# One pool of SBUF slots for the pieces of two weight matrices, with new orders for all engines

## The chip, the cores and the metric

The kernel runs on one core of one Trainium2 chip. A core has engines that each work through their own list of instructions in order: the tensor engine (PE), the vector engine (DVE), the scalar engine (ACT), GpSimd (POOL) and SyncE (SP), which in this kernel issues every DMA. The metric is the device time of the program in microseconds (us), lower is better. The kernel before took 477.4 us in the median of 6 runs, 476.62 to 478.06.

## The reference

Two layers with the same weights. A layer is attention over a sliding window, then an MLP that mixes along the sequence. All arrays are bf16; the sequence has 2048 rows, the model width is 512.

```python
def _A_ref(x, wqkv, wo):                       # D 512, 32 heads of 16, window 256
    qkv = (x @ wqkv).reshape(B, S, 3, H, Dh) ...
    scores = einsum("bhqd,bhkd->bhqk", q, k) * Dh ** -0.5
    mask = (idx[:, None] - idx[None, :] >= 0) & (idx[:, None] - idx[None, :] < W)
    p = softmax(where(mask, scores, -1e9))
    return einsum("bhqk,bhkd->bhqd", p, v) ... @ wo

def _B_ref(x, w1, b1, w2, b2):                 # w1 2048 x 1792, w2 1792 x 2048
    u = gelu(einsum("bsd,sf->bdf", layernorm(x), w1) + b1)
    y = einsum("bdf,fs->bds", u, w2) + b2
    return y.transpose(0, 2, 1)

x = A_x
x = x + _A_ref(layernorm(x), A_wqkv, A_wo)
x = x + _B_ref(layernorm(x), B_w1, B_b1, B_w2, B_b2)
...                                            # and both lines once more
```

## The kernel before

**Stages.** The sequence is cut in four chunks of 512 rows. `STEPS` (L258) lists the stages of each layer: `p` prepares a chunk (layer norm, in layer 1 also the last MLP's output rows it starts from, then q, k and v), `a` is its attention, `w` the output projection `wo`, `u` a part of the MLP's first product, `U` that product's last part with the gelu, and the `y` blocks are the second product (in layer 0 they are taken in by the next layer's `p`, in layer 1 they end the program, each followed by the DMA of its rows to the output).

**Attention** (`attention`, L903). PE makes scores in PSUM (L925); ACT takes their exponential into one of eight buffers `pt` (L937); DVE multiplies a mask in (L950, L953); PE multiplies with v (L971). DVE copies the product and the sums of a group of heads to a buffer `cs` (L1015). SP then brings the sums together (`rr`, L1017), moves half the product to the lower partitions (`cs`, L1021), and after DVE's reciprocal (L1024) writes it to DRAM (`rscr`, L1026) and reads it back spread over partitions (`md`, L1029). POOL multiplies both into `oT` (L1033), which `wo_block` (L1039) takes. The last group of each layer goes another way, with ACT (L998, L1000) and DVE (L1002). POOL also prepares k for the scores (`kbd`, L857).

**Layer norm** (`ln_block`, L753). DVE takes statistics (L757, L759), POOL the reciprocal deviation (L762, L764), DVE normalises to `xh_sb` (L768). PE transposes are read out by L803.

**The MLP.** `u_part` (L1075) multiplies pieces of w1 with `xh_sb` (L1089). A piece of w1 is 512 rows by 256 columns, 256 KB, loaded by `load_w1` (L1056, the DMA is L1058) to one of the four buffers of `w1b`. Its sum goes from PSUM to `ub` by a copy (L1098) for the first part of the sequence, by an addition (L1101) for later ones; gelu is L1104. `y_block` (L1109) multiplies pieces of w2 with the result (L1112); L1117 adds bias and residual. A piece of w2 is 256 rows by 256 columns, 128 KB, loaded by `load_w2` (L1064, the DMA is L1069) to one of the fourteen buffers of `w2b`, with at most 3 (layer 0) or 7 (layer 1) such loads under way.

**What sets the order.** Every step of this is recorded as an operation by `op` of the class `Graph` (L289), with what it reads and writes. `ORDER` (L21) holds one list of operation numbers for each engine, written out by hand or by a search. `follow` (L423) walks the five lists and gives each tile a slot of its pool, the moment an operation needs one; `reorder` (L493) then applies the small shifts of `MOVES` (L166), and `emit` (L502) writes each engine's instructions in that order with the semaphore waits that data and slots need. A list is strictly in order: an instruction that waits holds up all behind it on its engine, and a DMA that waits for a buffer holds up all later DMAs, since SP has a single list.

The two weight buffers take 8 KB and 14 KB of each partition:

```python
        w1b = sb("w1b", [P, NW1, 4, 256])                  # NW1 is 4
        w2b = sb("w2b", [P, 2 * NFT // W2F, W2F, 256])     # 14 buffers
...
        p_w1, p_w2, p_rscr = Pool("w1", NW1), Pool("w2", 2 * NFT // W2F), Pool("rscr", 3)
```

Of the kernel before, what the change touches and what calls it, by code (L numbers as in the profile page):

```python
# [11 lines left out]
P = 128  # L12
# [4 lines left out]
W2F, W2OUT = 2, (3, 7)  # L17
# [5 lines left out]
        11, 6, 13, 9, 14, 17, 10, 5, 16, 15, 8, 7, 69, 12, 71, 84, 85, 75, 73, 87, 77, 78, 81, 82, 93, 88, 185, 94,  # L23
        103, 104, 110, 96, 97, 111, 90, 91, 190, 100, 33, 107, 101, 108, 137, 195, 133, 114, 115, 135, 149, 200,
        139, 150, 217, 158, 152, 153, 222, 159, 205, 141, 227, 142, 155, 156, 232, 161, 162, 249, 254, 237, 166,
        146, 167, 147, 259, 169, 170, 174, 264, 175, 182, 183, 281, 177, 178, 329, 286, 331, 559, 333, 335, 561,
        291, 578, 269, 579, 296, 342, 343, 413, 337, 338, 366, 417, 367, 374, 375, 421, 425, 301, 563, 557, 356,
        429, 357, 351, 352, 445, 361, 362, 382, 449, 573, 574, 383, 453, 457, 433, 461, 570, 369, 370, 571, 477,
        481, 388, 389, 385, 465, 485, 386, 394, 489, 395, 391, 392, 493, 609, 610, 509, 606, 607, 513, 517, 497,
        653, 646, 654, 647, 521, 656, 657, 663, 525, 664, 593, 594, 743, 614, 615, 747, 529, 751, 588, 589, 755,  # L30
        345, 346, 348, 759, 349, 583, 584, 775, 565, 566, 779, 763, 783, 670, 671, 787, 598, 599, 649, 791, 650,
        677, 678, 807, 623, 624, 795, 811, 377, 378, 617, 667, 815, 618, 668, 819, 681, 682, 620, 823, 621, 601,
        602, 839, 626, 627, 843, 827, 847, 674, 675, 688, 851, 689, 684, 685, 855, 691, 692, 660, 948, 661, 702,
        703, 952, 705, 706, 859, 956, 712, 719, 720, 713, 960, 716, 717, 698, 964, 699, 726, 980, 727, 709, 968,
        984, 710, 730, 733, 734, 988, 731, 723, 992, 724, 880, 881, 996, 737, 738, 874, 1012, 875, 1016, 1000, 1020,
        740, 741, 695, 1024, 696, 871, 872, 1028, 877, 878, 1044, 1048, 1032, 1052, 1056, 900, 901, 917, 918, 1060,
        907, 908, 910, 911, 914, 924, 925, 903, 904, 915, 1064, 1065, 921, 922, 931, 928, 929, 1069, 1070, 932, 938,
        939, 1072, 1073, 935, 936, 1075, 1076, 1078, 945, 1079, 942, 1122, 946, 943, 1116, 1103, 1109, 1117, 1104,
        1129, 1123, 1110, 1135, 1124, 1130, 1131, 1105, 1106, 1111, 1118, 1112, 1136, 1137, 1119, 1125, 1148, 1138,
        1142, 1132, 1149, 1143, 1150, 1144, 1145, 1151, 1273, 1268, 1255, 1181, 1161, 1155, 1162, 1163, 1182, 1156,  # L40
        1183, 1164, 1168, 1157, 1169, 1170, 1158, 1187, 1184, 1171, 1174, 1175, 1269, 1176, 1177, 1274, 1188, 1189,
        1190, 1256, 1270, 1275, 1276, 1271, 1250, 1257, 1258, 1251, 1252, 1253, 1292, 1326, 1327, 1308, 1309, 1290,
        1288, 1328, 1286, 1302, 1303, 1294, 1314, 1321, 1297, 1316, 1406, 1299, 1305, 1300, 1306, 1319, 1311, 1411,
        1324, 1329, 1344, 1416, 1345, 1346, 1421, 1331, 1438, 1347, 1332, 1443, 1333, 1334, 1426, 1448, 1349, 1350,
        1453, 1351, 1470, 1352, 1362, 1475, 1376, 1458, 1377, 1480, 1364, 1485, 1379, 1380, 1366, 1534, 1502, 1368,
        1535, 1392, 1507, 1370, 1490, 1374, 1512, 1536, 1394, 1537, 1517, 1385, 1386, 1382, 1642, 1383, 1398, 1646,
        1400, 1522, 1650, 1404, 1388, 1654, 1539, 1540, 1658, 1541, 1542, 1674, 1552, 1662, 1678, 1553, 1554, 1572,
        1682, 1555, 1557, 1686, 1570, 1558, 1690, 1559, 1560, 1706, 1584, 1585, 1587, 1710, 1588, 1694, 1714, 1576,
        1574, 1620, 1718, 1612, 1606, 1722, 1610, 1604, 1738, 1600, 1582, 1742, 1746, 1726, 1622, 1578, 1750, 1590,
        1591, 1595, 1596, 1754, 1618, 1624, 1938, 1775, 1776, 1942, 1777, 1778, 1946, 1770, 1758, 1950, 1771, 1772,  # L50
# [4 lines left out]
        2169, 1900, 1904, 2173, 1901, 2189, 1911, 2177, 2193, 1912, 2066, 2197, 2070, 1916, 2201, 1917, 1919, 1920,  # L55
        2205, 2068, 2072, 2221, 1908, 1909, 2225, 2229, 2209, 1927, 1928, 2233, 1924, 1925, 2237, 1932, 1933, 1935,
        1936, 2241, 2242, 2091, 2093, 2103, 2101, 2096, 2250, 2246, 2252, 2113, 2111, 2108, 2248, 2106, 2098, 2118,
        2116, 2123, 2121, 2276, 2282, 2277, 2283, 2278, 2279, 2284, 2285, 2289, 2295, 2290, 2291, 2292, 2296, 2297,
        2298, 2315, 2316, 2321, 2322, 2317, 2318, 2323, 2308, 2309, 2302, 2303, 2310, 2304, 2311, 2324, 2334, 2305,
        2328, 2329, 2330, 2335, 2336, 2347, 2337, 2422, 2348, 2440, 2331, 2341, 2428, 2349, 2342, 2434, 2360, 2423,  # L60
        2343, 2354, 2361, 2355, 2350, 2356, 2429, 2344, 2441, 2362, 2363, 2435, 2452, 2424, 2357, 2436, 2446, 2430,
        2453, 2431, 2447, 2442, 2425, 2458, 2464, 2443, 2459, 2465, 2437, 2454, 2448, 2470, 2466, 2460, 2476, 2455,
        2477, 2471, 2461, 2449, 2467, 2478, 2472, 2479, 2488, 2473, 2482, 2483, 2489, 2490, 2484, 2500, 2501, 2494,
        2502, 2491, 2506, 2495, 2503, 2496, 2485, 2507, 2508, 2497, 2509, 2512, 2513, 2514, 2515,
    ),
    (
# [542 lines left out]
def bass_interleave_layers__sliding_block__mixer_token_mlp__prompt_kernel(  # L609
# [16 lines left out]
    NFT = F // P  # L626
# [4 lines left out]
    with es:  # L631
        sb = lambda name, shape, d=dt.bfloat16: es.enter_context(nc.sbuf_tensor(name, shape, d))
# [18 lines left out]
        w1b = sb("w1b", [P, NW1, 4, 256])  # L651
# [535 lines left out]
```

## Time and profile before

| what | us |
|---|---|
| median of 6 runs | 477.4 |
| the profiled execution | 477.06 |
| its span, first to last instruction | 475.3 |
| PE busy | 427.2 |
| DVE busy | 369.4 |
| ACT busy | 326.1 |
| POOL busy | 127.8 |
| share of 16 DMA engines that SP's queue used | 36.1% |

The mean granted clock of the tensor engine was 0.999. Busy time by stretch of the span:

| us of the span | length | PE | DVE | ACT | POOL | DMA share |
|---|---|---|---|---|---|---|
| 20 to 160 | 140 | 118.54 | 126.51 | 129.94 | 52.37 | 0.30 |
| 160 to 213 | 53 | 49.29 | 41.25 | 22.95 | 10.28 | 0.39 |
| 213 to 300 | 87 | 82.48 | 68.97 | 77.29 | 20.05 | 0.30 |
| 300 to 350 | 50 | 43.48 | 46.44 | 42.00 | 23.65 | 0.28 |
| 350 to 396 | 46 | 41.06 | 34.44 | 34.88 | 11.52 | 0.43 |
| 396 to 475 | 79 | 75.17 | 35.59 | 9.49 | 4.36 | 0.49 |

How to read it: an engine that is busy for nearly the whole of a stretch bounds it. In a group of the profile the name before the arrow is the output, the name behind it the input, L is the line of the kernel, and the idle time before an instruction is put down to what released it. A wait of an engine that is not on the chain costs nothing by itself.

### The profile page before, as it was taken

What the parts mean: (1) busy time and instruction counts of PE and PEld (TensorE: products, weight loads), DVE (VectorE), ACT (ScalarE), POOL (GpSimd) and SP (SyncE); (2) the same over time, 40 slices, a digit from 0 to 9 for tenths busy, and PEclk for the clock granted to TensorE, in tenths of its full rate; (3) what the DMA queues carried; (4) which work ended last, traced back from release to release, by engine and by line L of the source; (5) the groups of instructions that cost most, each with busy time, mean ns of one, the idle gap of its engine ahead of it and who ended that gap; (6) DMA issues with size and microseconds to landing.
All of it is one profiled execution on the core that took longest, in us unless ns stands there. A gap on an engine that the chain in (4) does not pass through costs nothing.

```text
span 475.3 us, 15635 instructions
## 1 busy us (share of the span) xinstructions
PE 427.2 (90%) x6764; PEld 206.6 (43%) x6830; DVE 369.4 (78%) x747; ACT 326.1 (69%) x371; POOL 127.8 (27%) x189
## 2 busy tenths in 40 slices
PE   7989877789887799999989998989978979999996
PEld 4454433354343344445454454445434434444442
DVE  7999979889988989574789888989985986941332
ACT  1999999799988951528998898888778862033000
POOL 3151454325612222010002714530591031200000
PEclk9999999999999999999999999999999999999999
DMA  8311431132443434331133513512316335533563
GB/s 243 91 51 48 110 118 50 49 92 64 127 122 108 138 115 121 102 101 34 36 99 77 139 41 106 147 51 51 83 51 178 98 109 171 146 98 113 165 192 130
DMA packets 83993, 49.47 MB, mean 104 GB/s; under 512 B 14676, under 2 KB 78164, under 8 KB 83924
## 3 DMA queue, kind: packets, MB, share of 16 engines
q1 hardware_dynamic: 83924, 48.46, 36.1%
q8 instruction: 54, 0.88, 0.8%
q14 instruction: 15, 0.12, 0.1%
HBM read 41.43 MB, written 2.59 MB: 93 GB/s over the span
## 4 chain that ended last, share of the span: by engine, by line
PE 61%; ACT 19%; DVE 13%; issue 2%; DMA 2%; POOL 1%; SPq 0%; POOLq 0%
PE PS L1112 18%; ACT pt L937 18%; PE PS L1089 16%; PE PS L836 5%; PE PS L925 5%; PE PS L971 5%; PE PS L1043 5%; PE PS L871 4%; DVE xh_sb L768 2%; DVE pt L950 2%; DVE cs L1015 2%; DVE pt L953 2%; PE PS L686 1%; DMA w1b<-in_B_w_dram 1%; DVE x_sb L1117 1%
## 5 line engine op out<-in xcount | busy, mean ns | idle before, releaser
L937 ACT ACTIVATE pt<-PS 128x1024 bf16<-128x1024 f32 (+1 forms) x304 | 283.4, 1038 | 30.8 <-PE PS L925 28.3
L1089 PE MATMUL PS<-xh_sb,w1b 128*128 128x512 bf16 x424 | 103.3, 380 | 9.8 <-ACT pt L937 2.5
L1112 PE MATMUL PS<-ub,w2b 128*128 128x512 bf16 x431 | 100.9, 379 | 1.8 <-issue 1.1
L925 PE MATMUL PS<-qT,kbd 32*128 32x64 bf16 (+4 forms) x1632 | 60.8, 243 | 19.1 <-ACT pt L937 8.1
L1089 PEld LDWEIGHTS PS<-xh_sb,w1b 128*128 128x128 bf16 x448 | 39.9, 98 | 58.8 <-issue 6.9
L1112 PEld LDWEIGHTS PS<-ub,w2b 128*128 128x128 bf16 x448 | 41.6, 98 | 51.3 <-issue 3.9
L1101 DVE TENSOR_TENSOR ub<-PS,ub 128x512 f32<-128x512 f32 x70 | 45.6, 683 | 22.9 <-PE PS L1089 22.8
L836 PE MATMUL PS<-xhT,wqkv 128*128 128x512 bf16 x238 | 59.5, 380 | 2.9 <-issue 2.2
L857 POOL TENSOR_SCALAR kbd<-stg,par 128x512 bf16<-128x512 bf16 x48 | 41.2, 869 | 69.8 <-DVE stg L803 69.6
L1033 POOL TENSOR_TENSOR oT<-cs,md 128x512 bf16<-128x512 f32 x30 | 40.3, 1346 | 69.1 <-DMA cs<-cs 49.2
L953 DVE TENSOR_TENSOR pt<-pt,ldm 128x1024 bf16<-128x1024 bf16 (+1 forms) x80 | 56.4, 714 | 2.6 <-ACT pt L937 2.6
L925 PEld LDWEIGHTS PS<-qT,kbd 32*128 32x128 bf16 x1632 | 23.3, 92 | 75.0 <-ACT pt L937 42.5
L1104 ACT ACTIVATE ub<-ub,bcol 128x512 bf16<-128x512 f32 x28 | 18.5, 712 | 46.7 <-DVE ub L1101 46.6
L1015 DVE COPY cs<-PS 128x512 f32<-128x512 f32 x60 | 38.8, 682 | 12.2 <-PE PS L971 11.9
L1117 DVE SCALAR_TENSOR_TENSOR x_sb<-PS,bcol,x_sb 128x512 bf16<-128x512 f32 x32 | 23.2, 745 | 31.2 <-PE PS L1112 31.1
L950 DVE TENSOR_TENSOR pt<-pt,ldm 128x512 bf16<-128x512 bf16 (+1 forms) x104 | 40.8, 413 | 5.0 <-ACT pt L937 4.9
L762 POOL TENSOR_SCALAR rstd<-agg 128x2 f32<-128x2 f32 (+1 forms) x36 | 8.9, 248 | 133.0 <-DVE agg L759 132.0
L757 DVE BATCH_NORM_STATS2 stats<-x_sb 128x6 f32<-128x512 bf16 x64 | 42.7, 681 | 0.7 <-DMA x_sb<-in_A_x_dram 0.4
L971 PE MATMUL PS<-pt,vt 64*18 64x64 bf16 (+4 forms) x3040 | 39.5, 242 | 3.7 <-ACT pt L937 2.3
L971 PEld LDWEIGHTS PS<-pt,vt 64*18 64x18 bf16 x3040 | 31.0, 84 | 14.1 <-ACT pt L937 4.8
L871 PE MATMUL PS<-wqkv,xhT 128*64 128x256 bf16 x512 | 34.7, 276 | 0.8 <-ACT pt L937 0.3
L1043 PE MATMUL PS<-wo_sb,oT 128*128 128x512 bf16 x121 | 31.5, 380 | 3.2 <-POOL oT L1033 2.0
(54 smaller groups left out, 315.0 us busy)
## 6 DMA issues: line engine op xcount, KB each, us to landing
w2b<-in_B_w_dram SPq DMA_DIRECT2D x112, 128.0 KB, 2.4
w1b<-in_B_w_dram SPq DMA_DIRECT2D x56, 256.0 KB, 3.4
md<-rscr SPq DMA_DIRECT2D x30, 256.0 KB
cs<-cs SPq DMA_DIRECT2D x120, 32.0 KB, 3.0
out_dram<-x_sb SPq DMA_DIRECT2D x16, 128.0 KB, 1.7
x_sb<-in_A_x_dram SPq DMA_DIRECT2D x3, 512.0 KB, 6.9
wqkv<-in_A_wqkv_dram SPq DMA_DIRECT2D x2, 384.0 KB
x_sb<-in_A_x_dram SPq DMA_DIRECT2D x4, 128.0 KB
```

Source lines behind the costliest of these rows:

```text
L836: mm_group(ft, 4, lambda e, c: e.matmul(PS[:, ft.slot, :], lhsT=wqkv[:, c, which * 512 + o * P:which * 512 + (o + 1) * P], rhs=xhT[:, tx.s ...
L871: last = e.matmul(PS[64 * hf:64 * hf + 64, ft.slot, sc * 256:(sc + 1) * 256], lhsT=xhT[:, tx.slot, c, tok:tok + 64], rhs=wqkv[:, c, 1024:1 ...
L925: last = e.matmul(PS[:, bank(r), c0 * 64:(c0 + nb) * 64], lhsT=kbd[32 * r:32 * r + 32, tkk.slot, jj, :, :].rearrange("p h n -> p (h n)"), ...
L937: return e.activation(pt[:, tp.slot, 2 * u:2 * u + 2, 0:n], PS[:, b0:b0 + 2, 0:n], ACTF.Exp, scale=SMSCALE)
L950: return e.tensor_tensor(v, v, msk.unsqueeze(1).to_broadcast([P, 4, w]), op=ALU.mult)
L953: return e.tensor_tensor(v, v, msk.unsqueeze(1).unsqueeze(1).to_broadcast([P, 4, k, w]), op=ALU.mult)
L971: last = e.matmul(PS[32 * r:32 * r + 18, tO[h].slot, q0 * 64:(q0 + nb) * 64], lhsT=vt[64 * h:64 * h + 64, tvv.slot, jj, 4 * o + r, :], rhs ...
L1015: op("vector", lambda e, tO=tO[h], tc=tc, h=h: e.tensor_copy(cs[:, tc.slot, h], PS[:, tO.slot, :]), reads=[tO[h]], writes=[(tc, h)], cost= ...
L1043: mm_group(ft, 4, lambda e, o, i=i, ft=ft: e.matmul(PS[:, ft.slot, :], lhsT=oT[:, tos[o][0].slot, i * P:(i + 1) * P], rhs=wo_sb[:, o, :], ...
L1089: out_ = e.matmul(PS[:, tu.slot, :], lhsT=w1b[:, tw.slot, s, tt * P:(tt + 1) * P], rhs=xh_sb[:, 4 * m + s, :], start=(n == 0 and s == 0), ...
L1101: op("vector", lambda e, tu=tu, ft=ft: e.tensor_tensor(uacc(ft), PS[:, tu.slot, :], uacc(ft), op=ALU.add), reads=[tu] + uk(ft), writes=uk( ...
L1112: mm_group(ft, NFT, lambda e, fc: e.matmul(PS[:, ft.slot, :], lhsT=w2b[:, tws[fc // W2F].slot, fc % W2F, k * P:(k + 1) * P], rhs=uT(fc), s ...
```

## The change

The two weight buffers become one, of the same 22 KB: `wb` has 22 slots of 1 KB per partition, and both kinds of pieces are drawn from one pool. A piece of w2 takes one slot, a piece of w1 two neighbouring ones. A stage that uses one kind only can so hold up to eleven pieces of w1 or 22 of w2 at a time. All five lists of `ORDER` and all of `MOVES` are new. The set of operations, their engines and their sizes are the same; which slot each tile gets, in this pool and in the others, follows from the new lists.

```diff
-        w1b = sb("w1b", [P, NW1, 4, 256])
-        w2b = sb("w2b", [P, 2 * NFT // W2F, W2F, 256])
+        NW = 2 * NW1 + 2 * NFT // W2F
+        wb = sb("wb", [P, NW, W2F, 256])
...
-        p_w1, p_w2, p_rscr = Pool("w1", NW1), Pool("w2", 2 * NFT // W2F), Pool("rscr", 3)
+        p_w, p_rscr = Pool("w", NW), Pool("rscr", 3)
...
         def load_w1(fb, s0):
-            tw = Tile(p_w1)
-            op("sync", lambda e: e.dma_start(w1b[:, tw.slot], w1v[:, s0:s0 + 4, fb * 256:(fb + 1) * 256]), writes=[tw],
+            tw = Tile(p_w, 2)
+            op("sync", lambda e: e.dma_start(wb[:, tw.slot:tw.slot + 2].rearrange("p a f n -> p (a f) n"),
+                                                  w1v[:, s0:s0 + 4, fb * 256:(fb + 1) * 256]), writes=[tw],
...
-                tw = Tile(p_w2)
+                tw = Tile(p_w, 1, "small")
                 w2_sent.append(op("sync", lambda e, f0=f0, tw=tw: e.dma_start(
-                    w2b[:, tw.slot], w2v[:, f0:f0 + W2F, i * 256:(i + 1) * 256]), writes=[tw], dma=True,
+                    wb[:, tw.slot], w2v[:, f0:f0 + W2F, i * 256:(i + 1) * 256]), writes=[tw], dma=True,
...
-                                    out_ = e.matmul(PS[:, tu.slot, :], lhsT=w1b[:, tw.slot, s, tt * P:(tt + 1) * P],
+                                    out_ = e.matmul(PS[:, tu.slot, :], lhsT=wb[:, tw.slot + s // 2, s % 2, tt * P:(tt + 1) * P],
...
-                PS[:, ft.slot, :], lhsT=w2b[:, tws[fc // W2F].slot, fc % W2F, k * P:(k + 1) * P], rhs=uT(fc),
+                PS[:, ft.slot, :], lhsT=wb[:, tws[fc // W2F].slot, fc % W2F, k * P:(k + 1) * P], rhs=uT(fc),
```

The lists hold numbers only. In words, the places of them that the prediction speaks of (a normalisation is L768, a row DMA is `rr`):

```
DVE, about 383 us of the span before
  before: cs copy, cs copy, normalise, mask, normalise x3, ub copy, reciprocal, ub copy, ub copy, mask, mask, ub copy
  after:  cs copy, cs copy, normalise, mask, ub copy, reciprocal, ub copy, mask, mask, mask, ub copy, normalise x2, ub copy, normalise
DVE, about 309 us
  before: mask, statistics x2, reciprocal, mask, cs copy x2, statistics, mask, y sum, normalise, statistics, reciprocal, mask, normalise x3, ...
  after:  mask, normalise, statistics x2, reciprocal, normalise x2, statistics, mask, cs copy x2, normalise x2, mask, y sum, mask, normalise, ...
DVE, about 341 us
  before: q cast, q cast, mask x2, normalise, k cast, k cast, mask, normalise x3, ...
  after:  q cast, mask x2, q cast, mask, k cast, k cast, mask, normalise x4, ...
PE, about 146 us
  before: scores, wo, wo, scores, u, u        after: scores, u, wo, wo, scores, u
SP, w2 of layer 0: 14 of its 56 pieces were issued in the first 165 us before; in the list after, none stands ahead of
  the transfers of layer 0's attention, which ended at 171 us
SP, w1: each load stands further ahead of its first use (the one used at 365.4 us was issued at 360.6)
```

## The prediction

> **What bounds the kernel now.** I read the busy row, the slices, the chain that ended last, the DMA issues, the tensor engine's waits and those of SP's queue, and then the chain and the vector engine's timeline at the places that these pointed to.
>
> ```profile
> PE 427.2 (90%) x6764; PEld 206.6 (43%) x6830; DVE 369.4 (78%) x747; ACT 326.1 (69%) x371; POOL 127.8 (27%) x189
> PE   7989877789887799999989998989978979999996
> DVE  7999979889988989574789888989985986941332
> ACT  1999999799988951528998898888778862033000
> PE 61%; ACT 19%; DVE 13%; issue 2%; DMA 2%; POOL 1%; SPq 0%; POOLq 0%
> w2b<-in_B_w_dram SPq DMA_DIRECT2D x112, 128.0 KB, 2.4
> w1b<-in_B_w_dram SPq DMA_DIRECT2D x56, 256.0 KB, 3.4
> ```
>
> A slice is 11.9 us. There are three regimes. In slices 2 to 14 (layer 0's attention) ACT's softmax exponentials sit at 9: ACT bounds, PE has room. At 180-220 us and from 400 us PE is at 9 and nothing else is: those stretches, the end of each MLP, run at PE's rate, so nothing can be had there, only lost. Between 220 and 400 us PE, DVE and ACT are all at 7 to 9, and short waits pass from one to the other. DMA is 2% of the chain.
>
> Next, what the two kinds of weight loads cost now. In the waits of PE and of SP's queue the columns are total us, times, longest:
>
> ```profile
> PE PS L1089 <- DMA w1b<-in_B_w_dram: 0.7, 1, 0.7
> PE PS L1043 <- POOL oT L1033: 2.0, 1, 2.0
> PE PS L1089 <- DVE ub L1098: 1.5, 1, 1.5
> PE PS L925 <- DVE stg L803: 1.8, 2, 1.6
> ```
>
> ```profile
> SPq L1058 <- PE PS L1089: 44.0, 25, 5.4
> SPq L1069 <- PE PS L1112: 29.8, 12, 15.9
> SPq L1069 <- PE PS L1089: 12.1, 4, 4.0
> ```
>
> SP stands 44.0 us at 25 w1 loads (L1058) until one of four buffers is read out; yet PE waits on a weight DMA once, for 0.7 us. SP's wait is nearly all hidden: on the 25 loads I find 0.7 to 2.9 us between landing (issue plus the row's 3.4) and first use. So the larger pool alone can return 0.7 us; whatever else comes must come from the new lists.
>
> **The change part by part.** No operation is added or removed: 806 tensor steps, 747 DVE, 371 ACT, 185 POOL operations and 409 DMAs stand in both lists, at the same sizes. Rewritten addresses cost nothing: same tiles, same instructions. What moves is order: PE by 1.5 places on average, ACT 0.24, DVE 2.1, POOL 4.2, SP 10.8.
>
> *The late w1 load.* The chain at 360 us:
>
> ```profile
> 360.59 0.58 SPq L1058
> 361.18 0.04 issue
> 361.22 4.75 DMA w1b<-in_B_w_dram
> ```
>
> The load was issued when a buffer came free at 360.6, landed at 366.0, and PE stood 0.67 us. In the new list it has a pair of slots free since 307 us; following SP's list with the times of before, it issues at about 356.5 and lands 5.6 us early. Gain 0.67 (bounds 0 and 0.67). The Trainium skill ("DMA: Bandwidth & Descriptors", Anatomy of one DMA) fits 2.0 us plus bytes at 436 GB/s, measured on the GpSimd path: 2.6 us for 256 KB. By it the load would have landed at 363.8, before PE needed it at 365.4, and the gain would be 0. The row here is 3.4 and this load's own piece 4.75; I take the trace.
>
> *DVE at 383-389 us.* PE stands 1.48 us from 387.32 until a copy L1098 has read out a PSUM bank. DVE's timeline, durations in the second column, and in the last line POOL's:
>
> ```profile
> 383.07 1.28 DVE L1015 COPY cs<-PS 128x512 f32<-128x512 f32 x2
> 384.27 0.40 DVE L768 TENSOR_SCALAR xh_sb<-x_sb,agg,rstd 128x512 bf16<-128x512 bf16 x1
> 384.59 0.68 DVE L953 TENSOR_TENSOR pt<-pt,ldm 128x1024 bf16<-128x1024 bf16 x1
> 385.19 2.95 DVE L768 TENSOR_SCALAR xh_sb<-x_sb,agg,rstd 128x512 bf16<-128x512 bf16 x3
> 388.07 0.68 DVE L1098 COPY ub<-PS 128x512 f32<-128x512 f32 x1
> 385.05 2.62 POOL L1033 TENSOR_TENSOR oT<-cs,md 128x512 bf16<-128x512 f32 x2 [0.94 <-DMA cs<-cs]
> ```
>
> The new list has after the two cs copies only one normalisation (L768) and one mask, then the copy, the reciprocal and the second copy; three normalisations follow later. 384.3 + 0.40 + 0.68 + 0.68 = 386.1, before PE arrives at 387.3: the gap closes. Of the four L768, two took 1.3, against 0.40, beside POOL's two products. The Trainium skill ("SBUF — State Buffer", SBUF: two separate sides) says that DVE and GpSimd share a port pair as an exclusive lock, the later one waiting out a whole instruction. The row agrees; by the rule the products may still block one of the two operations left in front, 1.3 more, 387.4, and the gain is 1.4; by the bare rows 1.48. I take 1.4. It must also survive the next wait: the products of the last group (L1033) ended at 397.8 and wo needs them. Their reciprocal also moves ahead, from 388.7 to about 386.6 (its row's DMA goes out at 384.4 in both, and SP waited 2.2 at most for such a row), so its row and md DMAs go out near 387 and 389.7 (SP behind two w1 loads whose slots are free at 387.1); md landed 4.6 us after issue (391.9 to 396.5), giving an end at 395.6. PE would reach wo at 397.0. It survives. Bounds 0 and 1.48.
>
> *DVE at 309-349 us.* PE stood 0.94 (320.1), 1.55 (344.9) and 0.64 (348.3), all behind DVE, which is busy 46.4 of 50 us at 300-350.
>
> ```profile
> 315.09 0.75 DVE L1117 SCALAR_TENSOR_TENSOR x_sb<-PS,bcol,x_sb 128x512 bf16<-128x512 f32 x1 [1.61 <-PE PS L1112]
> 317.48 2.10 DVE L768 TENSOR_SCALAR xh_sb<-x_sb,agg,rstd 128x512 bf16<-128x512 bf16 x3
> ```
>
> DVE idled 1.61 us before 315.09. Three normalisations that are not needed until 348 (run at 317.5, 322.8 and 328.3) stand before that idle time in the new list, 3 x 0.40 = 1.2 us put into a hole; POOL's rstd steps that they need are also moved ahead of two products. Another (344.78, 0.40) goes behind the casts that PE awaited at 344.9. Removed ahead of the three gaps: 1.6; a mask put ahead of the last cast takes back some 0.5. I take 1.1, bounds 0 and 3.1 (all three gaps).
>
> *PE at 146-149 us.* Its 2.0 us wait for POOL's product: the new list puts one u step (0.45 us) in front. ACT bounds this stage, so 0.2 (0 to 0.45). The product's inputs come no sooner: its rscr DMA waits for the reciprocal at 137.4 in both lists.
>
> *The moved w2 loads.* Before, 14 pieces of layer 0's w2 were loaded between 4 and 165 us; now all come from 171 us on, into slots that w1 gives up. SP spends the same issue time on them. Their cover is the slack: the first two issue at about 185 and are wanted at 191.7, the next at 190.9 and 192.9 for 197.8, so 2.5 us or more beyond the row's 2.4; in the last stage 1.9 us or more. I take 0; the price without cover is in the second rival. Queued behind them on SP are the row, cs and md transfers; most products' inputs land within 3 us of before, and the worst cases wait on POOL with 5 or more us to their wo. 0.
>
> *Everything else moved.* 21 PE gaps of over 0.5 us sum to 18.6, so 0.9 each. With DVE and POOL lists that changed throughout I allow for one new gap: +0.9 (0 to 4).
>
> Sum: 0.67 + 1.4 + 1.1 + 0.2 - 0.9 = 2.5 us. The span 475.3 becomes 472.8; the profiled run was 477.06, so 1.8 lie outside: 474.6. The median 477.4 is 0.3 above the profiled run: **474.9**.
>
> **Rivals.**
> 1. *Nothing to be had*: w1 was hidden already, the gaps wander to another engine. For: 0.7 us of direct wait; between 220 and 400 us three engines are within tenths. Against: the copy at 388 us is plainly behind work that can wait. Time 477.4, within 0.2% (0.95 us, about what a measurement here can tell from no change).
> 2. *Slower: w2 arrives late at the end of the MLPs.* PE has no idle time there (19.9 of 20 us at 180-200), so lateness is paid in full, once in each layer. It decides when a 128 KB piece needs over 4.9 us in layer 0 (2.5 + 2.4) or 4.3 in layer 1. For: 256 KB by md took 4.6 and one w1 load 4.75. Against: 2.4 is the row for 112 pieces. At 7 us it costs 2.1 + 2.7 = 4.8: 474.9 + 4.8 = 479.7.
> 3. *Slower: DVE's first 60 us.* It is at 9 in those slices, and the new list puts more layer-norm work ahead of the first masks. If ACT's exponentials starve for 3.5 us: 478.4. Against: eight score buffers lie between mask and exponential.
> 4. *Much faster*: SP, free of the 44 us, brings the products of layer 0 earlier and ACT regains 3.5 of its 10.1 idle us at 20-160: 471.4. Against: the products' inputs come at most 3 us sooner, and most wait for reciprocals.
>
> **How the numbers follow.** Forecast 0.50, own range 473.2 to 476.0 (the third part at 2.8 or at 0). First rival 0.14, second 0.15, third 0.13, fourth 0.08. Faster 0.58, same 0.14, slower 0.28. For 8 in 10 I leave out most of the fourth and the upper half of the second: 471.8 to 479.2.
>
> **What would show it.** SP's wait at w1 loads far below 44 us; no PE wait on a w1 DMA; no 1.5 us wait for L1098's copy at 386 us; under 2 us of PE gaps at 318-348 (3.1 now); PE at 19.9 of 20 at 180-220 and 400-460. PE waits on w2 in those two stretches would prove the second rival; ACT below 18.5 of 20 at 20-60 us the third. If the named gaps close and the time stays, new gaps must be seen elsewhere between 220 and 400 us.

## The result, and the profile after

The changed kernel takes 477.6 us (median of 33 runs), the kernel before beside it 478.2 us (70 runs). The ratio is 0.9966, with an interval of [0.9948, 0.9984]: faster by 0.34%, about 1.6 us. The medians are of all runs, while the ratio compares the fast ones alone, those within 1.5% of the fastest of the same kernel (24 of the 33 and 64 of the 70); the means of all runs give 0.998, 1.0 us. A second measurement on another chip, further down, gave 0.9985 [0.995, 1.002]; weighted by their intervals the two ratios give 0.997, some 1.4 us. The gain is thus some 1 to 1.6 us, while single runs of the changed kernel lie between 471.7 and 482.1.

The forecast had the sign right. Its time, 474.9 us, and its own range of 473.2 to 476.0 were missed; 477.6 lies inside the wider range of 471.8 to 479.2. Of the 2.7 us between, 0.8 is the kernel before, which stood at 478.2 in this measurement and not at 477.4; the rest is a forecast gain of 2.5 us of which 1 to 1.6 came, or 0.6 by the medians.

The profiled execution took 476.97 us, with a span of 475.2 at a clock of 0.999; that of before took 477.06 and had 475.3 and 0.999. The two executions shown are thus equally long, and the gain is not to be read from their spans. First the page of the changed kernel: busy row, slices, chain and the two kinds of weight loads.

```profile
PE 424.9 (89%) x6765; PEld 207.6 (44%) x6830; DVE 367.3 (77%) x747; ACT 326.2 (69%) x371; POOL 125.3 (26%) x189
PE   7889867789898699999999998889978999999996
DVE  7999879789998979564888898989986877853133
ACT  1999998799999950818998888789778872052000
PE 59%; ACT 19%; DVE 13%; DMA 3%; issue 3%; POOL 2%; SPq 1%; POOLq 0%
wb<-in_B_w_dram SPq DMA_DIRECT2D x56, 256.0 KB, 3.6
wb<-in_B_w_dram SPq DMA_DIRECT2D x112, 128.0 KB, 2.6
```

The regimes are those of before. PE, DVE and POOL are each busy some 2 us less (427.2, 369.4 and 127.8 before) with the same operations; what shortens them isn't shown. In PE's slices the change is visible as places: slice 6 (59 to 71 us) fell from 7 to 6, slice 14 (154 to 166) from 7 to 6 and slice 26 (297 to 309) from 9 to 8, while slice 33 (380 to 392) rose from 7 to 9. On the chain, DMA went from 2% to 3%.

Next, the changed kernel's waits: PE's, SP's and DVE's, with total us, times, longest. L1092 is the u step (L1089 before), L1101 the ub copy (L1098), L1060 the w1 load, L1072 the w2 load, and L566 a wait that is an instruction by itself.

```profile
PE PS L1092 <- DVE cs L1017: 4.5, 4, 2.5
PE PS L973 <- DVE x_sb L1120: 1.7, 1, 1.7
PE PS L1045 <- POOL oT L1035: 0.7, 1, 0.7
PE PS L927 <- DVE ub L1101: 0.5, 1, 0.5
...
SPq L1028 <- DVE rr L1026: 23.2, 10, 6.0
SPq L1072 <- PE PS L1115: 21.3, 9, 12.4
SPq L566 <- PE PS L1092: 9.7, 5, 3.2
SPq L1060 <- PE PS L1092: 8.9, 5, 4.0
...
DVE rr L1026 <- DMA rr<-cs: 2.7, 3, 1.2
```

What was forecast to go is gone. SP's 44.0 us at w1 loads are 8.9 at L1060, or 18.6 if the separate waits of L566 were all for w1. PE has no row for a weight DMA, none of 1.5 us for the ub copy, and its wait of 2.0 for POOL's product at 148 us is gone (the 0.7 in the row is the last product, at 398 us). What came instead is in the first two rows and the last: PE waits 1.7 us for the y sum (L1120) at 305.31 us, and 2.5 for cs copies at 86.46, where it had waited 1.9 before (for ACT by the profile) and waits 1.4 in e11, the same kernel; and DVE now waits for the DMA of the row of sums (L1019), 2.7 us in all, where before it had no such wait. Counted as the prediction counted them, PE's gaps of over 0.5 us are 26 with 22.2 us in all (25 with 19.0 in e11), where before had 21 with 18.6: most of the gaps that were named closed, and as many and more opened.

### The profile page after: what moved, and what is told of

Its sections match the earlier page's. It is cut to its first block, busy times and chain, and to the rows that moved or that the text cites. A ratio compares the mean times of both kernels' runs of the same rounds, so it can differ in the third digit from the quotient of the medians.

```text
span 475.2 us, 15639 instructions
## 1 busy us (share of the span) xinstructions
PE 424.9 (89%) x6765; PEld 207.6 (44%) x6830; DVE 367.3 (77%) x747; ACT 326.2 (69%) x371; POOL 125.3 (26%) x189
## 4 chain that ended last, share of the span: by engine, by line
PE 59%; ACT 19%; DVE 13%; DMA 3%; issue 3%; POOL 2%; SPq 1%; POOLq 0%
ACT pt L939 18%; PE PS L1115 18%; PE PS L1092 15%; PE PS L838 6%; PE PS L973 6%; PE PS L927 5%; PE PS L1045 4%; DVE pt L955 3%; PE PS L873 3%; DVE cs L1017 2%; DMA cs<-cs 2%; DVE stats L759 1%; DMA rr<-cs 1%; PE PS L688 1%; DVE pt L952 1%
## 5 line engine op out<-in xcount | busy, mean ns | idle before, releaser
L1092 PE MATMUL PS<-xh_sb,wb 128*128 128x512 bf16 x425 | 102.7, 380 | 8.7 <-DVE cs L1017 4.5
L1115 PE MATMUL PS<-ub,wb 128*128 128x512 bf16 x432 | 100.6, 379 | 1.7 <-issue 1.1
L1092 PEld LDWEIGHTS PS<-xh_sb,wb 128*128 128x128 bf16 x448 | 40.6, 98 | 56.5 <-issue 7.5
L1115 PEld LDWEIGHTS PS<-ub,wb 128*128 128x128 bf16 x448 | 41.8, 98 | 50.9 <-issue 3.6
L1120 DVE SCALAR_TENSOR_TENSOR x_sb<-PS,bcol,x_sb 128x512 bf16<-128x512 f32 x32 | 23.4, 746 | 37.7 <-PE PS L1115 37.6
L859 POOL TENSOR_SCALAR kbd<-stg,par 128x512 bf16<-128x512 bf16 x48 | 39.2, 825 | 46.3 <-DVE stg L805 44.5
L1107 ACT ACTIVATE ub<-ub,bcol 128x512 bf16<-128x512 f32 x28 | 18.6, 713 | 40.5 <-DVE ub L1104 40.4
```

The source lines that it names most:

```text
L1092: out_ = e.matmul(PS[:, tu.slot, :], lhsT=wb[:, tw.slot + s // 2, s % 2, tt * P:(tt + 1) * P], rhs=xh_sb[:, 4 * m + s, :], start=(n == 0 a ...
L1115: mm_group(ft, NFT, lambda e, fc: e.matmul(PS[:, ft.slot, :], lhsT=wb[:, tws[fc // W2F].slot, fc % W2F, k * P:(k + 1) * P], rhs=uT(fc), st ...
```

## How the comparison was made finer than the spans

The spans of single executions of one kernel differ by more than the change is worth: the changed kernel has 475.2 us in the trace above and 471.9 in that of run e11. So the tables below use another measure: the time from the end of one TensorE instruction to the end of another, both the same instructions of the program in each kernel, at cuts where all lists have done the same work. A value that recurs in every execution of one list and differs from that of the other list belongs to the list; one that jumps within a list does not. Most stretches recur to 0.05 us.

| stretch, us of before | list of before, executions without the edit | list after, executions without the edit | difference of the means |
|---|---|---|---|
| 7 to 55 | 47.66, 47.66, 47.86, 49.07 | 47.73, 47.35, 47.43 | -0.6 (-0.2 without the 49.07, where only the first 10 us are long) |
| 55 to 132 | 77.34, 76.67, 77.67 | 79.43, 78.42, 78.35 | +1.5 |
| 132 to 160 | 27.44, 27.38 | 26.33, 25.23, 26.44 | -1.4 |
| 160 to 201 | 41.45, 41.47, 41.44, 41.60 | 40.11, 41.05, 41.58 | -0.6, not steady |
| 201 to 273 | 71.59, 71.56, 71.56, 71.59 | 71.53, 71.52, 71.52 | -0.05 |
| 273 to 301 | 28.55, 28.81, 28.59, 28.59 | 29.84, 29.01, 29.26 | +0.7 |
| 301 to 312 | 11.08, 10.90, 11.14, 11.02 | 13.58, 12.78, 13.43 | +2.2 |
| 312 to 359 | 46.74, 46.75 | 45.53, 45.42, 45.42 | -1.3 |
| 359 to 387 | 27.79, 27.23, 27.62, 27.87 | 27.37, 27.92, 27.63 | 0.0 |
| 387 to 470 | 83.25, 83.24 | 81.86, 81.37 | -1.6 |

The executions are those of before and of e5, e6, e7 on the one side, and of the changed kernel, e11 and e9 on the other, each only where its own edit does not lie in the stretch. In 55 to 132 us, e7, e8, e10 and e12 are left out, in 132 to 160 e7 as well, and in 312 to 359 e6: the granted clock of TensorE dipped there. The differences, with -0.2 in the first line, sum to -0.8 us, beside the 1.0 to 1.6 that were timed. With two to four executions to a list they are indications, good to some tenths.

## The experiments

The reasons under test. Theory A: the forecast's local steps are real and the pool itself gives nothing. Its rivals change from batch to batch: B, that a gain of one place is absorbed at the next wait; C, that a reciprocal which DVE runs late makes the new losses by way of SP; and others, named where they are tested.

**The parts of the change by themselves (e1 to e4).** e1 has the shared pool and all five lists of before. e2 adds the new list of SP, e3 instead the new lists of the four compute engines. e4 has SP's new list and, of the others, only the stretches that the forecast speaks of. In these four kernels the final orders are written straight into the lists, so slots of all pools, not of the weights' alone, are given out anew; this is a side effect that e1 contains too. Their line numbers are smaller than those of before, since the shifts are gone.

```diff
-        p_w1, p_w2, p_rscr = Pool("w1", NW1), Pool("w2", 2 * NFT // W2F), Pool("rscr", 3)
+        p_w, p_rscr = Pool("w", NW), Pool("rscr", 3)
...
 ORDER = (
-    PE, DVE, ACT, POOL, SP of before     # final orders, shifts applied
+    e1: all five of before
+    e2: SP of after, four of before
+    e3: SP of before, four of after
+    e4: SP of after; of PE places 270-273, of DVE 550-597, 600-622 and 671-685, of POOL 125-170 of after; the rest before
-MOVES = (...)
+MOVES = ((), (), (), (), ())
```

> The shared pool with the five lists of the kernel before. Theory A (the pool by itself is worth nothing, since SP's waits for buffers were hidden; the time is made by the orders): within 0.2% of before, SP still standing long at w1 loads only where its list puts them late, the 1.5 us wait for the copy to ub and the 2.0 us wait for POOL's product still there. Theory B (deeper prefetch itself brings the time): 0.3% or more faster, about 1.5 us.

Measured: 478.78 us against 476.51, ratio 1.0048 [1.003, 1.0065]. The pool gives nothing: theory B falls, and A has the mechanism but not the number, for 0.48% slower is outside its 0.2%. With the old list, SP still stands at w1 loads.

```profile
SPq L967 <- PE PS L999: 37.8, 20, 5.2
```

The reason is that SP's list is in order. A slot that is free earlier is of use only if the load stands earlier in the list. The 0.5% that it costs can be the slots of the other pools as well as this one; e1 doesn't tell them apart.

> The shared pool and the new list of SP; PE, DVE, ACT and POOL in the order of before. Theory A: the late w1 load near 365 us is gone (0.6 us), and little else: 0 to 0.2% faster. Theory B: the whole measured gain of 0.34% or more, since the new orders of the other engines cost time. A third theory, that the new SP list makes row and product transfers late: 0.2% or more slower than before, with PE or DVE waits behind rr DMAs near 300 us.

Measured: 489.93 us, ratio 1.029 [1.0236, 1.0344]. SP's list alone costs 3% (0.5 of it as in e1), in the direction of the third theory and far more than it said. The trace of e2 shows where: SP's waits first, then DVE's.

```profile
SPq L926 <- DVE cs L924: 52.3, 8, 21.5
SPq L935 <- DVE rr L933: 41.6, 15, 8.1
...
DVE rr L933 <- DMA rr<-cs: 6.6, 3, 3.8
```

SP stands 41.6 us at the store of reciprocals (L935) for DVE to run them, and DVE stands 6.6 us at reciprocals for a row that SP has behind other transfers. Each list is in order and each waits for the other's.

> The shared pool, the new lists of PE, DVE, ACT and POOL, and SP's list of before. Theory A: the named gains (copy to ub near 388 us, product near 147 us) and the losses at 62-110 and 260-315 us are both there, within 0.3% of the changed kernel. If the losses come from SP's new list, they are gone here: 1% faster than before.

Measured: 498.86 us, ratio 1.0463 [1.0411, 1.0516]; neither expectation came. With the new compute lists and SP's old one, PE waits on weights, which is about half of the loss of 22 us:

```profile
PE PS L999 <- DMA wb<-in_B_w_dram: 10.0, 6, 3.1
```

So either half of the new lists costs 3% or 5%, while both together gain 0.3%. The five lists are matched to each other; a list can't be credited with a part of the gain.

> The shared pool, SP's new list, and of the other new lists only three stretches: PE's one u step ahead of wo at 146 us, DVE and POOL at 309-349 us, DVE at 383-393 us; all else in the order of before. Theory A: the gains read off the two traces (0.6 + 2.0 + 1.0 + 1.5) come without the losses: 4 to 5 us, 0.8 to 1.0% faster than before. If gains and losses only shift the same slack about, so that a gap closed in one place opens in the next: within 0.3% of before.

Measured: 483.33 us, ratio 1.0158 [1.0116, 1.02]; neither expectation came. Picking the stretches that the forecast names does not give their sum as long as SP's whole new list comes with them: SP's wait for reciprocals is 36.0 us here and DVE's for the rows 7.4, as in e2. Experiments after this one leave SP's list and all slots alone.

**Single stretches, in place (e5 to e7).** These put a few instructions of one engine's list in another order among the places that they already have. Nothing else moves, and every slot stays. The helper shifts the line numbers by 8.

```diff
         g.reorder(MOVES)
+        g.resort("vector", (2211, 2210, 2081, 2228, 1929, 2217, 1926, 2232, 2236, 2240, 1934, 2089, 2080, 1937, 2088))   # e5
```

> The kernel before, slots and all other lists untouched, with only VectorE's fourteen instructions of 383 to 389 us in the order that the change gives them (ub copy ahead of the normalisations and masks). Theory A (the gain of this step is local, 1.4 us as forecast, and nothing behind it absorbs it, since the MLP runs at TensorE's rate to the end): PE's 1.48 us wait for ub L1098 at 388.8 us is gone and the time is 475.0 to 475.6. Theory B (the step only gains where PE arrives as in the changed kernel; here the wait moves to the masks' readers): 476.3 to 477.

Measured: 476.06 us against 477.82, ratio 0.9961 [0.9937, 0.9985], 1.9 us (0.7 to 3.0). Theory A holds, by the ratio: PE's row for the ub copy of 1.5 us is gone from the trace, and 387 to 470 us take 81.71 instead of 83.25, 1.54 less, against 1.4 forecast. Fifteen instructions of one engine, in the kernel before, gain as much as the whole change.

```diff
+        g.resort("tensor", (737, 880, 881, 996))   # e6
```

> The kernel before with only TensorE's one u step (L1089) put ahead of the first wo step at 146 us. Theory A as forecast: 0 to 0.45 us less, because the wo step's input (POOL's product) comes when it did, so that u only fills part of the 2.02 us wait and what is behind it comes no sooner. Theory C (the lead of 2.1 us that the changed kernel showed here is not the step's gain but lag that this fixed wait absorbed): also 0 to 0.45 us. Theory D (the step itself is worth the 2.1 us that were seen): 474.3 to 475.

Measured: 478.65 us, ratio 1.0016 [0.9993, 1.004]. No gain that can be measured, so theory D (the u step alone is worth 2.1 us) falls. But the trace of e6 shows that the step did not get what it has in the changed kernel:

```profile
PE PS L1097 <- DMA w1b<-in_B_w_dram: 0.9, 1, 0.9
```

The wait for POOL's product is gone, and the moved step itself stands until 147.91 us for its piece of w1, which SP's old list issues at 144.69; in the change it runs at 147.13 with no such wait. So e6 bounds the step under the old list of SP, and not what the step and the earlier loads are worth together. TensorE came to this place 0.9 us later than in before, and of these it had made up 0.8 between 132 and 160 us. A and C can't be told apart by so little.

```diff
+        # e7: e5 and e6, and VectorE's places 600 to 622 (334 to 349 us) in the order of after
+        g.resort("vector", (1875, 1857, 1837, 1877, 1868, 1867, 2037))
+        g.resort("vector", (2023, 1869))
+        g.resort("vector", (1819, 2041, 2049, 1845, 2045))
+        g.resort("vector", (1853, 1847, 2053, 1873, 1881, 1880, 1872))
```

> The kernel before with the two edits above and VectorE's order of 334 to 349 us from the change as well (the second half of the stretch forecast at 1.1 us; the first half can't be moved without its slots). Theory A (the forecast's gains are real and add up when nothing else is moved): 1.4 + 0.2 + 0.5 = 2.1 us less, 474.0 to 474.8. Theory B (gains of one place are absorbed at the next fixed wait): at most 1 us less, 475.5 or more.

Measured: 475.86 us, ratio 0.996 [0.9938, 0.9982], 1.9 us (0.9 to 3.0). In the trace both DVE steps are there in full: 312 to 359 us take 45.98 instead of 46.74 (0.8, with 0.5 expected), and 387 to 470 take 81.70. That is 2.3 by stretches; the timed ratio can't tell it from the 1.5 of e5 alone. It agrees with theory A's 2.1, and does not exclude B.

**One late reciprocal (e8).** In the changed kernel, the trace at 283 to 306 us shows the loss of 301 to 312 as a chain through two queues. SP first, then the end of the chain that decides for this window, then DVE:

```profile
283.98 6.81 SPq L1028 DMA_DIRECT2D rscr<-rr  x2
...
294.09 1.32 SPq L1031 DMA_DIRECT2D md<-rscr  x2
...
295.95 0.56 SPq L1019 DMA_DIRECT2D rr<-cs  x1
```

```profile
295.95 5.12 DMA rr<-cs
...
301.09 0.35 DVE rr L1026
301.44 1.14 DVE pt L955 x2
302.58 1.41 DVE pt L952
303.99 0.60 DVE pt L955
304.59 0.67 DVE x_sb L1120
...
305.31 1.44 PE PS L973 x108
```

```profile
301.09 0.35 DVE L1026 RECIPROCAL rr<-rr 128x32 f32<-128x32 f32 x1 [1.03 <-DMA rr<-cs]
302.50 1.49 DVE L952 TENSOR_TENSOR pt<-pt,ldm 128x512 bf16<-128x512 bf16 x1
```

The reciprocal for SP's store stands in the new list behind seven casts and masks that followed it before (the eight of the expectation count it in), and ends at 290.43 (286.16 before). SP waits for it from 284, with all later transfers behind it; the next row of sums goes out at 295.95 instead of 293.07; DVE, in order, stands at the next reciprocal for it, with four masks and the y sum behind; PE waits 1.73 us for the y sum.

```diff
+        g.resort("vector", (1702, 1611, 1709, 1605, 1725, 1601, 1721, 1583))   # e8, in the changed kernel
```

> The changed kernel with one instruction moved: VectorE's reciprocal of 290 us (L1026) ahead of the eight casts and masks in front of it, so that it ends near 286.5 and SP, which stands 6.8 us at the store behind it (L1028, 283.98 us), is free 4 us sooner. Theory C (this one instruction makes the loss of 1.9 us at 299 to 304 us, through SP's next row and VectorE's wait of 1.03 us for it): PE's wait of 1.73 us for L1120 at 305.3 falls below 0.8, SP's row at L1019 is issued near 293, and the time is 1 to 1.9 us under the changed kernel's, 474.6 to 475.6 on this scale. Theory E (the loss comes from the masks and casts now ahead of L1120, not from SP): the wait stays and the time is within 0.5 us of the changed kernel's.

Measured: 476.68 us, ratio to before 0.9964 [0.9935, 0.9992], where the change has 0.9966. In the trace of e8, SP's stand at the store, its next row, and DVE's reciprocal without the wait ahead of it:

```profile
284.81 2.78 SPq L1036 DMA_DIRECT2D rscr<-rr  x2
...
294.37 0.56 SPq L1027 DMA_DIRECT2D rr<-cs  x1
```

```profile
301.63 0.32 DVE L1034 RECIPROCAL rr<-rr 128x32 f32<-128x32 f32 x1
```

```profile
PE PS L981 <- DVE x_sb L1128: 0.6, 1, 0.6
```

Theory C is right on the mechanism: SP is free 3.2 us sooner (287.6 against 290.8), DVE waits for no row at this place, and PE's wait for the y sum is 0.6 us, with 1.73, 0.99 and 1.65 in the three executions of the change's list. The stretch of 301 to 312 falls to 11.69 from 12.78 to 13.58. On the time it can't be upheld: 1.0 to 1.9 us less than the change was expected, and no difference is measured, with an interval of some 0.3% either way. A part of the local gain is lost just ahead: TensorE stands 0.54 us at 295.94 for nothing that the profile names, and the stretch of 273 to 301 takes 29.57, 0.2 more than the mean of the change. The trace also has a dip of the clock at 84 us, and dips hide such differences (last section): e8's four runs without one average 473.6 us, the change's ten 474.9; but the four of e12, which has this edit too, have 475.1. That is a hint of the gain and no more.

**The step at 385 us undone in the changed kernel, and the change again beside it (e9, e11).**

```diff
+        # e9, in the changed kernel: VectorE's places 671 to 685 in the order of before; e11 has no edit
+        g.resort("vector", (2228, 2210, 2211, 2080, 2232, 2088, 2089, 2081, 1929, 2217, 1926, 1934, 2240, 2236, 1937))
```

> The changed kernel with only VectorE's fifteen instructions of 383 to 389 us put back into the order of before. Theory A (the step at 385 us is worth all that the change gains; pool, w1 load, 309 to 349 and 146 us add up to nothing with the losses elsewhere): PE waits about 1.5 us for ub near 388 us again and the time is that of the kernel before, within 0.5 us (ratio 0.999 to 1.001). Theory B (the gain is spread, and the steps before 383 us carry at least half of it): ratio 0.9975 or less.

> The changed kernel as it is, on the chip of the two runs above, so that they can be compared with it directly. Every theory: 0.5 to 2.5 us under the kernel before, ratio 0.995 to 0.999. If its ratio differs from 0.9966 by more than 0.002, what is read from runs of different chips is no finer than that.

Measured: e9 480.44 us, ratio 1.005 [1.0015, 1.0084]; e11 477.72 us, 0.9985 [0.995, 1.002], both against 477.51. Without the 385 us step the change is slower than the kernel before. That goes further than theory A, whose range it misses, and B falls. PE's rows and DVE's timeline of e9:

```profile
PE PS L1100 <- DVE ub L1109: 2.5, 1, 2.5
```

```profile
388.06 2.16 DVE L778 TENSOR_SCALAR xh_sb<-x_sb,agg,rstd 128x512 bf16<-128x512 bf16 x3 [0.86 <-POOL rstd L774]
390.14 0.68 DVE L1109 COPY ub<-PS 128x512 f32<-128x512 f32 x1
```

The wait is 2.5 here and not 1.5, since in the changed kernel the normalisations ahead of the copy wait for POOL's rstd as well (0.86). From 387 to 470 us e9 takes 85.25, 3.4 to 3.9 more than the change and 2.0 more than before. Up to 1.7 of this is the clock, which fell to half for 3.41 us at 392.15, 1.3 us behind the wait; without it, some 1.7 to 2.2 more than the change and 0.3 more than before. With 0.8 that the stretches ahead of 387 us sum to in the table, this trace accounts for some 1.1 of the 2.4 us (0.7 to 4.0) by which e9 is slower than before; dips can be a part of the rest, since 10 of its 12 runs have one at least, against 13 of the 23 of before. The rest of the change, without this step, gains nothing and costs a little.

**Three mendings, then two (e10, e12).**

```diff
+        # e10 and e12, in the changed kernel, with e8's line:
+        g.resort("vector", (404, 412, 411, 499, 498, 512, 516))
+        # e10 alone:
+        g.resort("gpsimd", (312, 180, 365, 359))
```

> The changed kernel with three of its reorderings put right: the reciprocal of 290 us ahead of eight casts and masks (as in the run before), VectorE's two cs copies of 84.5 us ahead of two masks, and POOL's product of 69 us ahead of three kbd and vb products. Theory C (each is a local loss of 0.6 to 1.1 us on TensorE's path, and they add up): 2 to 3 us under the changed kernel, ratio to before about 0.991 to 0.993. Theory F (the lag that they cause is absorbed at the fixed waits behind them, at 147 us and 350 us, so that only what falls behind 360 us counts): within 0.7 us of the changed kernel's own ratio in this batch.

Measured: 486.19 us, ratio 1.0175 [1.0117, 1.0233]: 8 us slower where 2 to 3 faster was expected, by no theory. PE's waits and POOL's timeline of e10:

```profile
PE PS L846 <- POOL kbd L867: 4.0, 1, 4.0
```

```profile
67.44 1.26 POOL L1043 TENSOR_TENSOR oT<-cs,md 128x512 bf16<-128x512 f32 x1 [2.81 <-DMA cs<-cs]
68.69 1.36 POOL L867 TENSOR_SCALAR kbd<-stg,par 128x512 bf16<-128x512 bf16 x2
```

POOL, in order, stands 2.81 us for the product's cs transfer with the kbd products behind it, and PE's next projection is released by kbd, 4 us late. (What lies between the two, a staging slot, the cast into it and its PSUM bank, is from the code; the profile shows the ends.) In the change's list the kbd work fills that wait. I had read the order of POOL there as a fault, from 1.1 us that wo waits at 70.56; it hid a longer wait. The stretch of 65 to 74.5 us takes 14.85 us, with 9.5 to 10.3 in the changed kernel. The other part of the loss lies at 408.68, where wo waits 2.6 us for the last product, and in dips of the granted clock (0.83 at 60 to 80 us, 0.86 at 400 to 412): three in this trace, 13.7 us at half, so 6.8 us at most. They are not of this execution alone: the mean clock of e10's six runs is 0.986 to 0.993, that of e11's and e12's twelve each 0.993 to 1.0.

> The changed kernel with two of the three mendings of the run before: the reciprocal of 290 us ahead of eight casts and masks, and VectorE's two cs copies of 84.5 us ahead of two masks; POOL's order is left as the change has it. Theory G (the loss of 8 us in the run with three came from POOL's order alone: the product put first holds up kbd, and with it the staging slot that TensorE's next projection needs): no wait of TensorE for kbd near 70 us, the stretch of 65 to 74 us back at 9.3 to 10.3 us, 1 to 1.7 us under the changed kernel, ratio to before 0.993 to 0.9965. Theory H (the cs copies ahead of the masks are at fault): the time stays above 480.

Measured: 477.73 us against 477.83, ratio 1.0002 [0.9964, 1.0041]. Theory G is right on the cause: no wait for kbd, 65 to 74.5 us take 10.12, and the 8 us are gone with the one edit of POOL's list. The gain that it expected from the other two did not come. The reciprocal does there what it did in e8 (SP's stand 2.78 us, PE's wait for the y sum 0.6), but TensorE stands 0.95 us at 315.03 for nothing that the profile names (0.5 to 0.6 at this place in the change's own traces), and 301 to 312 us take 12.68. The cs copies start 2.0 us behind the reciprocal ahead of them instead of 2.5, since they now wait 0.6 for PE's product with v and not for the masks: that edit is worth 0.5 us at most.

None of the runs beats the change for certain. e5 and e7 equal it (0.9961 and 0.996) with 15 and 36 of VectorE's 747 instructions in another order (and four of TensorE's in e7), and without the shared pool.

## Why the prediction was right or wrong

*The late w1 load, 0.67.* The mechanism came: issued between 357.5 and 359.0 instead of 360.6 (356.5 was forecast), and no PE wait on a weight DMA. The gain did not. From 359 to 387 us the change takes what before took (27.6 in the mean of each). In the list of before, e5, which differs only from 383 us on, has no such wait in its trace either, and takes 27.23; e6 and e7 have none there too. And in the three executions of the change's list a wait that no engine accounts for stands at this place (0.63, 1.18 and 0.89 us, at 361 to 363; 0.93 in e7), which is looked at in the last section. I took one wait of one execution for a property of the list. The lower bound, 0, was the answer. The trace's row for 256 KB loads, on which the sum preferred 3.4 us to the Trainium skill's fit of 2.6 ("DMA: Bandwidth & Descriptors", Anatomy of one DMA), stands at 3.6 after: the row was rightly preferred, but decided nothing.

*DVE at 383 to 389, 1.4.* Right: 1.5 us alone in the kernel before (e5), 1.4 and 1.9 in the two traces of the change. Here is DVE's timeline of the changed kernel:

```profile
385.58 0.88 DVE L770 TENSOR_SCALAR xh_sb<-x_sb,agg,rstd 128x512 bf16<-128x512 bf16 x1
386.38 0.68 DVE L955 TENSOR_TENSOR pt<-pt,ldm 128x1024 bf16<-128x1024 bf16 x1
386.98 0.68 DVE L1101 COPY ub<-PS 128x512 f32<-128x512 f32 x1
388.84 0.35 DVE L1026 RECIPROCAL rr<-rr 128x32 f32<-128x32 f32 x1 [1.18 <-DMA rr<-cs]
```

The one normalisation left ahead of the copy took 0.88 instead of 0.40, beside a product of POOL's that had 0.7 us to go when it began: 0.5 of the 1.3 that the lock could have cost (last section). The reciprocal behind it waited 1.18 us for its row, which the forecast had at 386.6 without a wait; the last product then held wo for 0.7 us in this execution and for 0.3 at most in e11. "It survives" was nearly so.

*DVE at 309 to 349, 1.1.* Right: 1.3 us by the stretch 312 to 359, of which e7 got 0.8 from the second half alone. It would be 1.0 more but for a larger wait at 350.76, inside the stretch, where PE stands 1.60 us (0.64 at this place before). The profile puts it down to ACT's exponential, which ended at 350.49; the last of four normalisations for this step ended at 350.45, so the work put off was late next.

*PE at 146 to 149, 0.2.* The u step alone, under SP's old list, gives nothing that can be measured (e6). The change gains 1.4 between 132 and 160 us all the same. POOL's product, whose inputs "come no sooner", ended at 147.16 instead of 148.2 although TensorE came to this place 0.8 us later than before, and the step found its piece of w1 loaded, for which it stood 0.9 us in e6. But the gain can't be booked to the new lists: e1, with all orders of before and the shared pool, takes 25.7 us from 132 to 160, as little as the change (25.2 to 26.4, and 27.4 in before). Its cause stays open.

*The moved w2 loads, 0.* Right. In the change, 14 more w2 loads follow 171 us, and PE has no row for a weight DMA; from 201 to 273 us the two kernels take 71.5 and 71.6, and from 400 to 460 us PE is busy 59.7 of 60 in both.

*Everything else moved: one new gap, 0.9.* This is the step that failed, in size. By the stretches, the new gaps cost 1.5 (55 to 132) + 0.7 (273 to 301) + 2.2 (301 to 312) = 4.4 us, in place of 0.9 and over the bound of 4. What was not forecast either gives back some 0.6 at 160 to 201 that isn't steady, 0.2 ahead of 55, and the 1.4 at 132 to 160: 2.2 are left. The named steps brought 0 for the w1 load + 1.6 + 1.3 = 2.9 in place of 3.4. The net by stretches is 0.7 to 0.8, the timed one 1.0 to 1.6, and 2.5 was forecast. The prediction looked for such gaps between 220 and 400 us; 2.9 of the 4.4 lie there, and 1.5 ahead of it. The term was taken as a count (one gap of mean size), though the two lists could be followed at any place: both lists were on hand, and at 290 us they show SP's store behind a reciprocal that had been moved behind seven other instructions. I had asked for the loads that SP issues when their slots were free and when PE needed them, and of the rows and stores only whether the products' inputs came late, not whether DVE, which waits for them in order, would stand with masks and the y sum behind it. With the reciprocal back (e8, e12), PE's wait at this place is 0.6 instead of 1.0 to 1.7, so this move makes 0.4 to 1.1 of the 2.2; the rest of this stretch, and most of the other new gaps, I can place but have not taken apart.

*The rivals.* The first (nothing to be had) is refuted by e5, which got 1.9 us at one place. Its picture of gaps that wander is what happened to the rest of the forecast, and its time of 477.4 is nearer to the measured 477.6 than the forecast's 474.9. The second (w2 late) isn't seen. Of the third, DVE's first 60 us cost nothing (7 to 55 us are a little shorter), but 55 to 132 cost 1.5: its mechanism, ACT's exponentials starving, is not seen: ACT is busy 38.5 of the 40 us from 20 to 60, and 38.8 before. The fourth (SP's freedom bringing the products sooner) is seen at 147 us with 1.0; I found no other place.

## What to carry to other kernels

Where every engine works through a list in order, look for the places where a queue waits for an engine that waits for that queue; here SP's stores behind DVE's reciprocals and DVE's reciprocals behind SP's rows. Any reordering must be followed through both, and a half of such a change can cost 3 to 5% while the whole gains 0.3%. A larger buffer gives nothing until the loads stand earlier in the list. A wait that is seen behind one instruction may be what another order was hiding: before it is moved, see what would stand behind it in its new place. And where executions of one program differ by 0.7%, compare the time between equal instructions over several executions, not spans, and look at the granted clock of each before its stretches are compared.

## What the hardware showed

Two executions of the same instructions (the change and e11) differed by 3.3 us in span at clocks of 0.999 and 0.998, gathered in stretches with cross-engine waits; those that TensorE bounds recur to 0.01 us. In other executions the granted clock fell to half for 3.41 us, or for twice that, as in e8 for 6.83 us from 84.13 on. Over the wider windows here the mean is 0.92 and 0.88:

```profile
74.00:86.00 12.00, 7.31 (x183) 0.92 0.43 116
86.00:106.00 20.00, 18.05 (x398) 0.88 0.39 93
```

(The columns are length, PE busy, granted clock, DMA share, GB/s.) e8 takes 81.87 us from 55 to 132, with 78.4 to 79.4 in the changed kernel without a dip. All 17 dips of the traces began within a wait of TensorE of 0.55 to 3.5 us or at most 1.4 us behind one; but waits as long pass without a dip (2.5 us at 86.46 in the change), and no run shows what decides.

The mean clock of most runs is on record, and a dip of 3.41 us lowers it by 0.0036, so the runs can be sorted by it. Of the runs of before beside e5 to e8, 29 of 67 have no dip and take 476.5 us in the mean, and 27 have one and take 478.6. Of the change, 10 of 34 have none and take 474.9, and 21 have one and take 478.4; of e11, 6 of 12 have none and take 475.5, against 476.3 in 10 of 23 of before. So a dip takes more than the change gains, and how many fall into the runs moves a median by as much; the gain is seen in the runs without one, 0.8 us in e11 and some 1.6 in the change (the clocks of the 70 runs beside it are not on record).

TensorE stands at a few places for nothing that the profile names ("issue"), 0.35 to 2.05 us each. In the three executions of the change's list one is at 361 to 363 us, and its size varies where no edit does (0.63, 1.18, 0.89). PE's timeline of the changed kernel, and its instruction queue on the page:

```profile
363.37 0.35 PE L927 MATMUL PS<-qT,kbd 32*128 32x256 bf16 x5 [0.63 <-issue]
```

```profile
q8 instruction: 54, 0.88, 0.8%
```

54 packets in a span are one in 8.8 us. In eleven traces (before, the change, e1 and e5 to e12) there are 30 such waits of 0.35 us or more, and in each the last packet of this queue began 2.2 to 3.1 us before the wait ended, which chance would not do. The Trainium skill ("Runtime: NRT & Kernel Launch", Instruction fetch mechanics) says that an engine's instructions are loaded in blocks of 16 KiB while it runs, at a cost that is mostly hidden; 0.88 MB in 54 packets agree with the size. That these waits are late code is therefore likely, but no run varied it. They were not in the forecast, and at 0.5 to 1 us each they are as large as its terms.

The same normalisation took 0.40 us alone and 0.88 or 1.15 beside a product of POOL's (385.58 in the change, 385.45 in e9). The forecast weighed such a lock of the two engines with a whole instruction's wait. In the eleven traces 79 normalisations took over 0.6 us, and each of them ended 0.14 to 0.15 us behind an instruction of POOL's (386.46 and 386.31 in the change): it waits out what is left of that instruction, which is the whole only where both begin together. The rule that the prediction cites agrees, and its 1.3 us is the worst case.
